# New landing times and biases in a hand-planned instruction order, and gate logits in other buffers, in a gated attention and GEGLU kernel

## Chip, cores and metric

One core of one Trainium2 chip runs the whole program. The metric is the device time of one execution in microseconds (us), lower is better. A profile of one execution gives the "span", from the first to the last instruction on the core; the execution's own time is a little longer than its span. The engines are TensorE (PE; its weight loads are listed as PEld), VectorE (DVE), ScalarE (ACT), GpSimd (POOL) and SyncE (SP). In this program POOL and SP mostly issue DMA transfers; their queues are written POOLq and SPq.

## The reference

The input x is [1, 2048, 1024] in bf16. Two branches read it and a sigmoid gate mixes them row by row:

```
g = sigmoid((x * gate_w).sum(-1))                       # one number for each row
# A: 32 heads of 32; window of 8 keys at distance 2 (s, s-2, ..., s-14)
q, k, v = x @ wqkv                                      # wqkv 1024 x 3072
a = softmax(q . k[window] / sqrt(32)) . v[window] @ wo  # wo 1024 x 1024
# B: GEGLU, 3584 hidden features
b = (gelu(x @ w_gate) * (x @ w_up)) @ w_down
out = g * a + (1 - g) * b
```

## The kernel before

**Tiling.** The 2048 rows are four chunks of 512, handled as two pairs (0, 1) and (2, 3). Each of the three large products (QKV, the FFN's up and gate, and w_down together with wo) is made by one level of a seven-product scheme in the manner of Strassen and Winograd: sums and differences ("forms") of quarters of the operands are made on DVE, and PE makes seven products of them where a plain split needs eight. Partial results pass between the products through PSUM banks: ACT copies a bank to another bank ("seed") or to a float buffer (tags "m5" and "u2", two buffers each), and DVE adds a bank to such a buffer.

**Forms.** T1, T2, T4 are forms of x, made by `x_forms` (T1 on L515, in two halves for the first pair; T2 on L519; the others on L521 and L522). `qkv_forms` (L761) makes the forms of wqkv, once for each pair. `wforms` (L494) makes the forms of w_up and w_gate, which POOL stores to DRAM (L503) for the second pair. `preps` makes the "down sums", forms of w_down and wo: loads by L387 into one of three staging areas in the FFN's hidden buffer hT, four DVE sums to a group (L468 to L473), four stores by POOL (L478). `down_forms` (L1328) makes the forms of the hidden activations.

**PE's stream**, `main`: QKV of the first pair (Q by `first_pair`, matmuls on L595 and L826; K and V by `qkv_pair`, L826); the FFN of chunks 0 and 1 (`ffn`, L1198, 28 blocks of features, f); the down products of chunk 0 (L1367); QKV of the second pair in the order Q, V, K; four blocks of the second FFN; the down products of chunk 1; the rest of that FFN; the down products of chunks 2 and 3. In `qkv_pair` a bank is released to PE by DVE's sums L891 and L901 and by ACT's copies L862, L874, L884 and L912. In `ffn` the sum L1265 (up half) and the sum L1286 (before the second GELU) do so, and L1247 multiplies by the GELU.

**Gate.** `gate(c)` makes the gate's logits by eight small matmuls (L928). For chunk 0 DVE transposes the bank directly (L942); for chunk 1 ACT first copies it (L936) and DVE transposes the copy (L939). The transposed logits `zt` lie in a tile of tag "u2" for chunks 0 and 1, until DVE has picked out the 16 needed columns (`zq`, L946). The second of the first pair's ACT copies into "u2" (L667) needs that tile.

**Attention** runs on DVE, half a chunk (256 rows) at a time, beside PE's products: scores as window products (L999) and additions (L1005); a transposing DMA on SP's queue (L1068); the softmax (L1079 to L1122); ACT spreads the weights (L1128); two transposing DMAs turn them back (L1137); products with v (L1146) and their sums (L1156 to L1164).

**Parking.** The second pair's q, k and v of chunk 3 have no room of their own yet. They are written into the hidden buffer hT, stored to DRAM by POOL (`park`, L781, 1 MB each), and loaded back by SP later (`moves`, L787). The space in hT is overwritten in the meantime by `down_forms` of chunk 1 (L1328) and by the second FFN.

**What sets the order.** Every operation is an `Op` in one of eleven streams (Python generators), and the class `Weave` merges them into one fixed order for each engine by a list scheduler with a cost model: it repeatedly takes the stream whose next operation has the smallest estimated start plus bias. Nothing of that model runs on the chip, except that the instructions of each engine are chained in the order chosen; on the chip each then waits for its semaphores, and whatever stands behind it on its engine waits too. The rule in `run`:

```
b = s[0] if op.due is None or t + self.AHEAD < op.due else 0.0
b = b if op.bias is None else op.bias
if best is None or t + b < best[0]:
    best = (t + b, t, s, op)
```

`s[0]` is the stream's bias and `t` the estimated start; an operation with a due time loses its stream's bias once that time is near. A DMA's estimated landing (`_emit`) is

```
self.pipe = max(self.pipe, t + 1.4) + nbytes / self.RATE
op.end = self.pipe + 1.3 + (op.tail if op.tail > 1.0 else 0.0)
```

so that `tail` is an extra landing time in the model only.

Of the kernel before, what the change touches and what calls it, by code (L numbers as in the profile page):

```python
# [9 lines left out]
ALU = mybir.AluOpType  # L10
# [4 lines left out]
P = 128  # L15
# [4 lines left out]
SC = 512  # L20
# [23 lines left out]
class Weave:  # L44
# [4 lines left out]

    LAT = 0.1  # L50
    RATE = 370e3
    AHEAD = 12.35

    def __init__(self, nc, tc):
        self.nc, self.tc = nc, tc
# [99 lines left out]
def kernel(  # L155
# [65 lines left out]
    QVK = (0, 2, 1)  # L221
    GMAJ = False
    TORD = (0, 1, 4, 5, 2, 3, 6, 7)
    DUE = (80.01, 302.59)
    XR = FT - 12
    ring = persist.tile([P, NG, GR], BF16)
    banks = [psum.tile([P, SC], F32, name=f"ps{i}") for i in range(8)]
# [145 lines left out]
    def load_prep(i0):  # L373
        n = min(2, NPREP - i0)
        kind, src, nr = ("d", B_w_down, FH) if i0 < FH else ("o", A_wo, NTH)
        r0 = i0 if kind == "d" else i0 - FH
        si = i0 // 2 % NSTG

        def fn():
            st = stage(si)  # L380
            for h, r in ((0, r0), (1, nr + r0)):
                if kind == "d":
                    v = src[r * P:(r + n) * P, :].rearrange("(k p) (h n) -> p k h n", p=P, h=2)
                else:
                    v = AP(src.tensor, src.offset + r * D, [[NT * D, P], [D, n], [NW, 2], [1, NW]])
                for k in range(n):
                    nc.sync.dma_start(out=st[:, 2 * h + k], in_=v[:, k])  # L387
        return Op("SP", (4 * n * P * NW * 2, 2.0 * n), fn, [("preps", i0 - 2 * NSTG)] if i0 >= 2 * NSTG else [("qkv", 1, 0, t) for t in range(NT)] if si == 2 else [("pt", KH - 1, 1)] if si == 1 else [("seeded",)],
                  key=("prep", i0))

    def load_block(sup, b, first=()):
        c0, c1 = b * FB * P, (b + 1) * FB * P
# [68 lines left out]
    def preps():  # L461
        for i0 in range(0, NPREP, 2):
            kind, r0, n = ("d", i0, min(2, FH - i0)) if i0 < FH else ("o", i0 - FH, min(2, NPREP - i0))
            st = stage(i0 // 2 % NSTG)
            b11, b12, b21, b22 = st[:, 0:n, 0], st[:, 0:n, 1], st[:, 2:2 + n, 0], st[:, 2:2 + n, 1]
            fo = (b11, b22, b12, b21)
            t = tt(n * NW)
            f0 = dve(t, lambda: V(out=b11, in0=b12, in1=b11, op=ALU.subtract), due=DUE[0] + 2.82 * i0, deps=[("prep", i0), ], lag=1.0)  # L468
            yield f0
            yield dve(t, lambda: V(out=b12, in0=b22, in1=b12, op=ALU.subtract), due=DUE[0] + 2.82 * i0)  # L470
            f1 = dve(t, lambda: V(out=b22, in0=b22, in1=b11, op=ALU.subtract), [f0], due=DUE[0] + 2.82 * i0)
            yield f1
            last = dve(t, lambda: V(out=b21, in0=b21, in1=b22, op=ALU.subtract), [f1], due=DUE[0] + 2.82 * i0)  # L473
            yield last
            dd = (ddram if kind == "d" else odram)[:].rearrange("f p (k n) -> p f k n", n=NW)
            for f in range(4):
                o = Op("POOL", (n * P * NW * 2, 0.8),
                       lambda f=f: nc.gpsimd.dma_start(out=dd[:, f, r0:r0 + n, :], in_=fo[f]), [last],  # L478
                       key=("preps", i0) if f == 3 else None)
                yield o  # L480
            if i0 + 2 == FH:
                w.done[("stored", "d")] = o
            if i0 + 2 == NPREP:
                w.done[("stored", "o")] = o

    def wforms():
        t = tt(GR)
        for b in range(NBLK):
            ops = []
            for f, x_, y_, op in ((0, "U21", "A22", ALU.add), (2, "A11", "U21", ALU.subtract), (1, 0, "A11", ALU.subtract),  # L490
                                  (3, "A12", 1, ALU.subtract)):
                def go(f=f, x_=x_, y_=y_, op=op, b=b):
                    g = ring_take(("w", 0, b, f))
                    nc.vector.tensor_tensor(out=g, in0=ring[:, held[("w", 0, b, x_)], :],  # L494
                                            in1=ring[:, held[("w", 0, b, y_)], :], op=op)
                o = dve(t, go, [("w", 0, b, x_), ("w", 0, b, y_)], key=("w", 0, b, f), lag=0.5, pre=ring_pre,
                        due=DUE[0] + 11.51 * b)
                yield o
                if f == 2:
                    ring_give(("w", 0, b, "U21"), o)  # L500
                if NSUP > 1:
                    yield Op("POOL", (P * GR * 2, 0.6),
                             lambda b=b, f=f: nc.gpsimd.dma_start(out=fdram[b][:, f * GR:(f + 1) * GR],  # L503
                                                                  in_=ring[:, held[("w", 0, b, f)], :]),
                             [("w", 0, b, f)], key=("ws", b, f))

    def x_forms():
        t = tt(KH * SC)
# [221 lines left out]
    def qkv_forms():  # L730
        for sup in range(NSUP):
            c = 2 * sup
            t = tt(D)
            for which in QVK if sup else (0, 1, 2):
# [13 lines left out]
                for f in range(4):  # L748
                    for kt in range(0, KH, 2):
                        def go(f=f, kt=kt, which=which, c=c):  # L750
                            if f != 2:
                                ring_take(("wqf", c, which, f, kt // 2))
                            o, x_, y_, op = ((lambda: form(0, kt), lambda: raw(kt, 1), lambda: raw(kt + KH, 1), ALU.add),
                                             (lambda: form(1, kt), lambda: form(0, kt), lambda: raw(kt, 0), ALU.subtract),
                                             (lambda: raw(kt, 1), lambda: raw(kt, 0), lambda: raw(kt, 1), ALU.subtract),
                                             (lambda: form(3, kt), lambda: raw(kt + KH, 0), lambda: form(1, kt),
                                              ALU.subtract))[f]
                            args = [z() for z in (o, x_, y_)]
                            m = max(len(z) for z in args)
                            for o1, x1, y1 in zip(*[parts(z, m) for z in args]):  # L760
                                V(out=o1, in0=x1, in1=y1, op=op)  # L761
                        dep = raw_keys(c, which, (kt, kt + KH, kt + 1, kt + 1 + KH))
                        if f in (1, 2):
                            dep.append(("wq", c, which, 0, kt))
                        elif f == 3:
                            dep.append(("wq", c, which, 1, kt))
                        if f == 2 and not sup and which == 0:
                            dep.append(("xf", 0, 1))
                        op = dve(t if c < 2 and which != 1 else t + 0.065, go, dep, key=("wq", c, which, f, kt), lag=0.5,
                                 pre=ring_pre if f != 2 else None,  # L770
                                 bias=(0.05, -0.75)[which == 0] if which < 2 and not sup else None,
                                 due=DUE[1] + 13.63 * QVK.index(which) + 2.54 * f if sup else 0.0)
                        yield op
                        w.done["wq", c, which, f, kt + 1] = op

# [3 lines left out]
    def park(which):  # L779
        r = NT * (0, 2, 1)[which]  # L780
        return Op("POOL", (P * NT * SC * 2, 1.0), lambda: nc.gpsimd.dma_start(  # L781
            out=parked[which].rearrange("p (t s) -> p t s", s=SC), in_=hrow[:, r:r + NT, 0:SC]),
            [("tmp", which, t) for t in range(NT)], key=("parked", which))

    def moves(c):
        def back(which, dst, deps):
# [133 lines left out]
    def gate(c):  # L920
# [9 lines left out]
                                     tile_position=(0, 32 * q), skip_group_check=True)  # L930
        o = pe(KT // 4 + 1, go, ([free] if free else []) + dx + [("gcol",)], key=("z", c))
        yield o
        zt = work.tile([P, SC], F32, tag="m5" if c > 1 else "u2", bufs=2, name="zt")
        if c == 1:
            za = work.tile([P, 2 * SC], BF16, tag="gl", bufs=3, name="za")[:].bitcast(F32)
            e = act(0.48, lambda: nc.scalar.copy(out=za, in_=banks[i][:]), [o])  # L936
            yield e
            bank_give(i, e)
            e = dve(0.63, lambda: nc.vector.transpose(out=zt[:], in_=za), [e])  # L939
            yield e  # L940
        else:
            e = dve(0.63, lambda: nc.vector.transpose(out=zt[:], in_=banks[i][:]), [o], bias=-2.0 if c < 2 else None)  # L942
            yield e
            bank_give(i, e)
        zq = small.tile([P, SC // 32], F32, tag="zq", bufs=2, name="zq")
        e = dve(0.1, lambda: nc.vector.tensor_copy(out=zq[:], in_=zt[:].rearrange("p (b j) -> p b j", j=32)[:, :, 0]), [e],  # L946
                key=("zq", c))
        yield e
        zc = small.tile([P, NST], F32, tag="zc", bufs=2, name="zc")
# [528 lines left out]
    def main():  # L1478
# [20 lines left out]
        for part in down(3):  # L1499
            yield from part  # L1500

    w.run([(0.0, main()), (0.0, loads()), (0.0, late_x()), (0.0, moves(3)), (0.6, wforms()), (0.0, down_forms()), (0.02, x_forms()), (1.95, qkv_forms()),
           (1.53, preps()), (0.1, attention()), (0.28, scores())])
    LOG.append(w)


# [28 lines left out]
```

## Time and profile before

| quantity | value |
|---|---|
| three timed runs | 722.01, 721.44, 719.56 us |
| their median | 721.44 us |
| profiled execution, own time | 720.26 us |
| its span on core 0 | 718.5 us |
| granted TensorE clock | 1.00 |
| DMA | 176.84 MB, mean 246 GB/s |

How to read the profile. The page's first part gives the busy time of each engine, its share of the span and its instruction records (a small share of matmul records can be missing). Rows of a timeline read: start in us, busy us, engine, line and operation, output <- inputs by the program's names, shape, number of instructions merged, and in brackets the idle time of the engine before them with what ended it. In a table by stretches each engine has its busy time and records. "DMA share" is the mean busy share of the core's 16 DMA engines. The chain of waits lists, back from the end, what each step waited for. In a DMA's row, "us to landing" counts from its issue. "PE", "DVE" and so on with a line number mean the instruction issued at that line of the kernel; in the changed kernel lines from about L930 on are two further down.

### The profile page before, as it was taken

How to read it: one execution, taken by the hardware profiler on the slowest of the kernel's cores; microseconds unless marked ns; L12 is line 12 of the kernel's file. 1: busy time of each engine (PE TensorE's matmuls, PEld its weight loads, DVE VectorE, ACT ScalarE, POOL GpSimd, SP SyncE). 2: the span in 40 equal slices, each digit the busy share in tenths (PEclk: the TensorE clock that was granted, in tenths of full speed). 3: DMA queues.
4: the chain of work that ended last, by engine and by line, in shares of the span. 5: the costliest groups of instructions: out<-in, count | busy, mean ns of one | idle time of the engine just before them, and what ended most of it. 6: DMA issues, size and time to landing. Idle time of an engine off the chain costs nothing.

```text
span 718.5 us, 9947 instructions
## 1 busy us (share of the span) xinstructions
PE 708.3 (99%) x3305; PEld 345.7 (48%) x3371; DVE 610.9 (85%) x888; ACT 326.9 (45%) x556; POOL 73.9 (10%) x130
## 2 busy tenths in 40 slices
PE   9999999999999999999989999999999999999998
PEld 5566544444444444456654444444444444444444
DVE  4999999999999979899779988899999997839300
ACT  5353675555675522153455323258556655310111
POOL 0030333343211000100000000100000000001000
PEclk9999999999999999999999999999999999999999
DMA  9952989996896799944558899996658756999993
GB/s 271 371 178 74 267 294 306 355 353 203 217 260 213 220 246 345 337 164 146 105 167 272 279 308 358 303 307 186 179 144 190 177 163 159 316 315 354 305 326 111
DMA packets 182835, 176.84 MB, mean 246 GB/s; under 512 B 56320, under 2 KB 138880, under 8 KB 182656
## 3 DMA queue, kind: packets, MB, share of 16 engines
q1 hardware_dynamic: 173168, 145.53, 69.9%
q0 software_dynamic: 9328, 30.42, 11.6%
q8 instruction: 26, 0.43, 0.2%
q10 hardware_dynamic: 288, 0.26, 0.1%
q14 instruction: 25, 0.20, 0.1%
HBM read 132.65 MB, written 31.46 MB: 228 GB/s over the span
## 4 chain that ended last, share of the span: by engine, by line
PE 84%; issue 10%; DVE 3%; DMA 2%; POOL 1%; ACT 0%; DVEq 0%; POOLq 0%; ACTq 0%
PE ps L1198 45%; PE ps L1367 26%; PE ps L826 10%; DMA parked<-hT 1%; PE ps L595 1%; DMA ring<-dforms 1%; DMA ring<-in_B_w_down_dram 1%; PE ps L322 1%; POOL out_dram L1400 0%; PE ps L552 0%; DVE ring L494 0%; DVE u L1286 0%; DVE xbuf L1091 0%; DVE hT L1265 0%; DVE tf L519 0%
## 5 line engine op out<-in xcount | busy, mean ns | idle before, releaser
L1198 PEld LDWEIGHTS <-ring 128*128 128x128 bf16 x1568 | 153.3, 98 | 185.3 <-issue 0.9
L1198 PE MATMUL ps<-lend,ring 128*128 128x512 bf16 x879 | 210.9, 379 | 0.9
L1198 PE MATMUL ps<-tf,ring 128*128 128x512 bf16 x658 | 162.9, 379 | 0.9
L1367 PE MATMUL ps<-ring,hT 128*128 128x512 bf16 (+1 forms) x704 | 159.6, 375 | 0.9
L1367 PEld LDWEIGHTS <-hT 128*128 128x128 bf16 x722 | 70.6, 98 | 82.6 <-DVE xbuf L1005 0.4
L1146 DVE TENSOR_TENSOR xbuf<-xbuf,lend 128x2048 bf16<-128x2048 bf16 x64 | 78.0, 1222 | 15.3 <-DMA xbuf<-xbuf 15.2
L826 PEld LDWEIGHTS <-ring 128*128 128x128 bf16 x512 | 64.7, 127 | 48.5 <-issue 3.1
L999 DVE TENSOR_TENSOR xbuf<-qo,lend 128x2048 bf16<-128x2048 bf16 x64 | 77.0, 1222 | 0.6 <-ACT lend L884 0.6
L1005 DVE TENSOR_TENSOR xbuf<-xbuf 128x2048 bf16<-128x2048 bf16 x56 | 68.4, 1221 | 0.2
L826 PE MATMUL ps<-tf,ring 128*128 128x512 bf16 x250 | 58.1, 379 | 2.5 <-DVE lend L891 1.8
L826 PE MATMUL ps<-lend,ring 128*128 128x512 bf16 x251 | 57.6, 379 | 0.3
L1230 ACT COPY ps<-ps 128x512 f32<-128x512 f32 x56 | 32.0, 572 | 50.9 <-PE ps L1198 50.7
L1274 ACT ACTIVATE gl<-ps 128x512 bf16<-128x512 f32 x56 | 33.6, 600 | 38.3 <-PE ps L1198 37.2
L1408 ACT ACTIVATE ost<-ps,omg 128x512 bf16<-128x512 f32 x15 | 10.3, 688 | 88.4 <-PE ps L1367 88.4
L1367 PE MATMUL ps<-ring,qo 128*128 128x512 bf16 (+1 forms) x193 | 49.1, 375 | 0.2
L1400 POOL DMA_DIRECT2D out_dram<-ost x24 | 13.0, 541 | 338.9 <-ACT ost L1408 249.7
L1247 DVE TENSOR_TENSOR hT<-hT,gl 128x1024 bf16<-128x1024 bf16 x56 | 38.6, 689 | 9.9 <-ACT hT L1240 9.7
L1290 ACT ACTIVATE gl<-u 128x512 bf16<-128x512 f32 x56 | 35.4, 632 | 22.6 <-DVE u L1286 22.0
L503 POOL DMA_DIRECT2D fforms<-ring x56 | 30.7, 549 | 140.8 <-DVE ring L494 134.6
L1286 DVE TENSOR_TENSOR u<-ps,u 128x512 f32<-128x512 f32 x56 | 38.6, 689 | 2.7 <-PE ps L1198 2.5
L1156 DVE TENSOR_TENSOR xbuf<-xbuf 128x2048 bf16<-128x2048 bf16 x32 | 39.1, 1222 | 0.0
L1282 ACT COPY u<-ps 128x512 f32<-128x512 f32 x56 | 32.8, 586 | 13.4 <-PE ps L1198 13.2
(127 smaller groups left out, 681.4 us busy)
## 6 DMA issues: line engine op xcount, KB each, us to landing
ring<-dforms SPq DMA_DIRECT2D x112, 256.0 KB, 4.9
ring<-in_B_w_down_dram SPq DMA_DIRECT2D x84, 256.0 KB, 5.1
ring<-in_B_w_gate_dram SPq DMA_DIRECT2D x56, 256.0 KB, 4.6
fforms<-ring POOLq DMA_DIRECT2D x56, 256.0 KB, 5.6
ring<-fforms SPq DMA_DIRECT2D x56, 256.0 KB, 4.3
ring<-in_B_w_up_dram SPq DMA_DIRECT2D x42, 256.0 KB, 5.2
ring<-in_A_wqkv_dram SPq DMA_DIRECT2D x32, 256.0 KB, 4.0
ring<-oforms SPq DMA_DIRECT2D x32, 256.0 KB, 5.6
```

What stands on the lines that cost most here:

```text
L826: nc.tensor.matmul(banks[bk][:], lhsT=lhsT, rhs=rhs[:, kt, :], start=(start and kt == 0), stop=(kt == KH - 1), skip_group_check=True)
L999: V(out=w3(box[t]), in0=q_b, in1=k_w, op=ALU.mult)
L1005: V(out=w3(box[0]), in0=w3(box[0]), in1=w3(box[t]), op=ALU.add)
L1146: return dve(tt(n), taking(("p", t), lambda: V(out=w3(box["p", t]), in0=w3(box["ab"]), in1=v_w, op=ALU.mult)), [("qkv", c, 2, t), abo] + ( ...
L1156: V(out=p0.rearrange("p (u n) -> p u n", u=2), in0=lo, in1=hi, op=ALU.add)
L1198: nc.tensor.matmul(banks[bk][:], lhsT=wv[:, k, fl * P:(fl + 1) * P], rhs=rhs[:, k, :], start=(start and k == 0), stop=(k == KH - 1), skip_ ...
L1247: yield dve(tt(2 * SC), lambda hv=hv, gv=gv: nc.vector.tensor_tensor(out=hv, in0=hv, in1=gv, op=ALU.mult), [e, ev[f, "g1"], ev[f, "g2"]], ...
L1274: nc.scalar.activation(out=gl[f][:, r1 * SC:(r1 + 1) * SC], in_=banks[A[f]][:], func=ACT.Gelu_apprx_tanh)
L1282: nc.scalar.copy(out=u2[f][:], in_=banks[Bk[f]][:])
L1286: e = dve(tt(SC, True), lambda f=f: nc.vector.tensor_tensor(out=u2[f][:], in0=banks[Dk[f]][:], in1=u2[f][:], op=ALU.add), [o, ev[f, "u2"]])
L1290: ev[f, "g2"] = act(0.54, lambda f=f: nc.scalar.activation(out=gl[f][:, r2 * SC:(r2 + 1) * SC], in_=u2[f][:], func=ACT.Gelu_apprx_tanh), [ ...
L1367: nc.tensor.matmul(banks[bk][:, o0:o0 + cols[1] - cols[0]], lhsT=l, rhs=wv[:, i, cols[0]:cols[1]], start=(start and k == 0), stop=(q == la ...
```

## The change

Numbers of the order model: the look-ahead `AHEAD`, the first due times `DUE`, the slopes of due times, stream biases, and an extra landing time (`tail`) for the loads of the down sums, the stores of FFN weight forms, and the park stores. The operations themselves, their engines and their data stay the same, except that some of L761's forms of 1024 columns are issued as two of 512 where their two operands no longer lie at one distance, and that the buffers and one dependency of the gate are edited: the transposed logits of chunks 0 and 1 go to a tile of tag "gl" (three buffers, otherwise for GELU outputs and results), and chunk 0's transpose waits for the second half of T1, ("xf", 0, 1). The diff, with the first of the four like lines of `preps`:

```diff
-    AHEAD = 12.35
+    AHEAD = 14.59
...
-    DUE = (80.01, 302.59)
+    DUE = (80.05, 297.87)
...
@@ load_prep @@
-                  key=("prep", i0))
+                  key=("prep", i0), tail=3.5)
...
@@ preps @@
-            f0 = dve(t, lambda: V(out=b11, in0=b12, in1=b11, op=ALU.subtract), due=DUE[0] + 2.82 * i0, deps=[("prep", i0), ], lag=1.0)
+            f0 = dve(t, lambda: V(out=b11, in0=b12, in1=b11, op=ALU.subtract), due=DUE[0] + 1.87 * i0, deps=[("prep", i0), ], lag=1.0)
...
@@ wforms @@
-                        due=DUE[0] + 11.51 * b)
+                        due=DUE[0] + 12.15 * b)
...
-                             [("w", 0, b, f)], key=("ws", b, f))
+                             [("w", 0, b, f)], key=("ws", b, f), tail=1.4)
...
@@ qkv_forms @@
-                                 bias=(0.05, -0.75)[which == 0] if which < 2 and not sup else None,
-                                 due=DUE[1] + 13.63 * QVK.index(which) + 2.54 * f if sup else 0.0)
+                                 bias=(0.19, -0.6)[which == 0] if which < 2 and not sup else None,
+                                 due=DUE[1] + 19.19 * QVK.index(which) + 3.94 * f if sup else 0.0)
...
@@ park @@
-            [("tmp", which, t) for t in range(NT)], key=("parked", which))
+            [("tmp", which, t) for t in range(NT)], key=("parked", which), tail=2.6)
...
@@ gate @@
-        zt = work.tile([P, SC], F32, tag="m5" if c > 1 else "u2", bufs=2, name="zt")
+        zt = work.tile([P, SC], F32, tag="m5", bufs=2, name="zt")[:] if c > 1 else \
+            work.tile([P, 2 * SC], BF16, tag="gl", bufs=3, name="ztg")[:].bitcast(F32)
...
-            e = dve(0.63, lambda: nc.vector.transpose(out=zt[:], in_=banks[i][:]), [o], bias=-2.0 if c < 2 else None)
+            e = dve(0.63, lambda: nc.vector.transpose(out=zt, in_=banks[i][:]), [o] + ([("xf", 0, 1)] if c == 0 else []),
+                    bias=-2.0 if c < 2 else None)
...
@@ main @@
-    w.run([(0.0, main()), (0.0, loads()), (0.0, late_x()), (0.0, moves(3)), (0.6, wforms()), (0.0, down_forms()), (0.02, x_forms()), (1.95, qkv_forms()),
-           (1.53, preps()), (0.1, attention()), (0.28, scores())])
+    w.run([(0.0, main()), (0.0, loads()), (0.0, late_x()), (0.0, moves(3)), (0.6, wforms()), (0.0, down_forms()), (0, x_forms()), (1.89, qkv_forms()),
+           (0.12, preps()), (0.03, attention()), (0.23, scores())])
```

More of the change, by code (lines that the diff above doesn't have):

```diff
@@ L467, in preps @@
             t = tt(n * NW)
-            f0 = dve(t, lambda: V(out=b11, in0=b12, in1=b11, op=ALU.subtract), due=DUE[0] + 2.82 * i0, deps=[("prep", i0), ], lag=1.0)
+            f0 = dve(t, lambda: V(out=b11, in0=b12, in1=b11, op=ALU.subtract), due=DUE[0] + 1.87 * i0, deps=[("prep", i0), ], lag=1.0)
             yield f0
-            yield dve(t, lambda: V(out=b12, in0=b22, in1=b12, op=ALU.subtract), due=DUE[0] + 2.82 * i0)
-            f1 = dve(t, lambda: V(out=b22, in0=b22, in1=b11, op=ALU.subtract), [f0], due=DUE[0] + 2.82 * i0)
+            yield dve(t, lambda: V(out=b12, in0=b22, in1=b12, op=ALU.subtract), due=DUE[0] + 1.87 * i0)
+            f1 = dve(t, lambda: V(out=b22, in0=b22, in1=b11, op=ALU.subtract), [f0], due=DUE[0] + 1.87 * i0)
             yield f1
-            last = dve(t, lambda: V(out=b21, in0=b21, in1=b22, op=ALU.subtract), [f1], due=DUE[0] + 2.82 * i0)
+            last = dve(t, lambda: V(out=b21, in0=b21, in1=b22, op=ALU.subtract), [f1], due=DUE[0] + 1.87 * i0)
             yield last
@@ L938, in gate @@
             bank_give(i, e)
-            e = dve(0.63, lambda: nc.vector.transpose(out=zt[:], in_=za), [e])
+            e = dve(0.63, lambda: nc.vector.transpose(out=zt, in_=za), [e])
             yield e
         else:
-            e = dve(0.63, lambda: nc.vector.transpose(out=zt[:], in_=banks[i][:]), [o], bias=-2.0 if c < 2 else None)
+            e = dve(0.63, lambda: nc.vector.transpose(out=zt, in_=banks[i][:]), [o] + ([("xf", 0, 1)] if c == 0 else []),
+                    bias=-2.0 if c < 2 else None)
             yield e
@@ L945, in gate @@
         zq = small.tile([P, SC // 32], F32, tag="zq", bufs=2, name="zq")
-        e = dve(0.1, lambda: nc.vector.tensor_copy(out=zq[:], in_=zt[:].rearrange("p (b j) -> p b j", j=32)[:, :, 0]), [e],
+        e = dve(0.1, lambda: nc.vector.tensor_copy(out=zq[:], in_=zt.rearrange("p (b j) -> p b j", j=32)[:, :, 0]), [e],
                 key=("zq", c))
```

## The prediction

> **What bounds the kernel now.** I read the totals first, then PE's timeline, then for each hole in it the engine named as its releaser. The totals give, for each engine, busy us, share of the span and records:
>
> ```profile
> span 718.5 us, 9947 instructions
> PE 708.3 (99%) x3305; PEld 345.7 (48%) x3371; DVE 610.9 (85%) x888; ACT 326.9 (45%) x556; POOL 73.9 (10%) x130
> ```
>
> PE is the bound, and its clock is 1.00 throughout. The change leaves PE's 3357 matmuls and their order as they are, so time can only come from, or go into, PE's pauses. PE's timeline shows full stretches of 512-column matmuls starting every 0.216 us. A late start is therefore: next start, less last group's start, less issued matmuls times 0.216. (A record in fifty is missing: the "x23" at 361.37 is 24 matmuls by the code.) All pauses that count, in three windows of that timeline (start, us, what, idle before and releaser):
>
> ```profile
> 14.95 1.05 PE L826 MATMUL ps<-tf,ring 128*128 128x512 bf16 x4
> 16.41 1.02 PE L826 MATMUL ps<-tf,ring 128*128 128x512 bf16 x4 [0.41 <-DVE tf L515]
> ...
> 23.12 1.03 PE L826 MATMUL ps<-lend,hT 128*128 128x512 bf16 x4
> 24.47 2.75 PE L826 MATMUL ps<-lend,hT 128*128 128x512 bf16 x12 [0.32 <-ACT u2q L667]
> ```
> ```profile
> 199.25 1.03 PE L1198 MATMUL ps<-tf,ring 128*128 128x512 bf16 x4
> 200.30 1.89 PE L1198 MATMUL ps<-lend,ring 128*128 128x512 bf16 x8
> 202.30 1.89 PE L1198 MATMUL ps<-tf,ring 128*128 128x512 bf16 x7
> ```
> ```profile
> 361.37 5.34 PE L826 MATMUL ps<-lend,ring 128*128 128x512 bf16 x23
> 368.51 1.89 PE L826 MATMUL ps<-tf,ring 128*128 128x512 bf16 x8 [1.79 <-DVE lend L891]
> ```
>
> At 16.41 four matmuls from 14.95 end their turn at 14.95 + 4 x 0.216 = 15.81: 0.60 late. At 24.47: 23.98 was due, 0.49 late. At 200.30: 200.11 was due, 0.19. At 202.30: 202.03 was due, 0.27. At 368.51: 361.37 + 24 x 0.216 = 366.55 was due, 1.96. Together **3.51 us**; the rest of the span offers nothing to gain. Three of the DVE's timelines show the causes:
>
> ```profile
> 15.07 0.72 DVE L942 STREAM_TRANSPOSE zt<-ps 128x512 f32<-128x512 f32 x1 [0.18 <-PE ps L928]
> 15.71 0.65 DVE L515 TENSOR_TENSOR tf<-lend,lend 128x1024 bf16<-128x1024 bf16 x1
> ```
> ```profile
> 121.28 0.69 DVE L468 TENSOR_TENSOR hT<-hT 128x1024 bf16<-128x1024 bf16 x1
> 123.48 0.69 DVE L470 TENSOR_TENSOR hT<-hT 128x1024 bf16<-128x1024 bf16 x1 [1.50 <-DMA hT<-in_B_w_down_dram]
> ...
> 128.95 1.22 DVE L1146 TENSOR_TENSOR xbuf<-xbuf,lend 128x2048 bf16<-128x2048 bf16 x1
> ```
> ```profile
> 365.63 2.22 DVE L1328 TENSOR_TENSOR hT<-hT 128x1792 bf16<-128x1792 bf16 x2 [3.81 <-DMA parked<-hT]
> 367.77 1.28 DVE L891 TENSOR_TENSOR lend<-ps,m5q 128x512 bf16<-128x512 f32 x2
> ```
>
> **The change, part by part.** The new biases and landing times are no instructions; what counts is the order that they give, read from the two built programs.
>
> *Gate logits.* The gate's transpose L942 stood between the two halves of the first form T1; it now waits for the second half. That half follows the first at the DVE's pace of 0.60: 14.20 + 0.60 = 14.80, done near 15.45, before PE's 15.81. So 0.60 goes. Late next could be T2 (L519), moved back by the transpose, not in sum: both still precede it, it ends at about 17.3, and PE reaches its first T2 matmul at about 18.2. The gate's bank comes free at 16.2 instead of 15.8; its next taker is due at 17.3. The second pause: ScalarE's copy L667 stood until 23.83 for the DVE's zq copy L946 at 23.58 (waits: 2.5 us in one), since logits sat in one of the two "u2" buffers which L667 fills. They now sit in "gl", whose three buffers are otherwise used by GELU, first after 66 us. So 0.49 goes. Sum 1.09.
>
> *Cost of split forms.* Seven of L761's 1024-wide sums become pairs of 512-wide ones (888 to 895 DVE records). By their rows (0.689 and 0.422 mean) that is at most 7 x (2 x 0.422 - 0.689) = 1.09 us of DVE, between 24 and 40 us. There the DVE has holes (0.57 at 40.83, two of 0.17 after) and PE none that it causes; I cost it at 0, and at up to 1.09 if a form in that stretch is the one PE is waiting for.
>
> *Down sums (L468 to L473) in FFN 1.* From 66 us the DVE is the crowded engine (columns: PE busy and records, PEld, DVE, ACT, POOL, clock, DMA share, GB/s):
>
> ```profile
> 66.00:86.00 20.00, 19.89 (x93) 11.60 (x94) 19.88 (x28) 9.44 (x18) 3.82 (x7) 1.00 0.65 178
> 86.00:124.00 38.00, 37.84 (x175) 17.22 (x177) 36.19 (x67) 26.64 (x45) 15.31 (x24) 1.00 0.98 308
> 124.00:206.00 82.00, 81.44 (x372) 36.95 (x379) 81.27 (x124) 49.29 (x88) 25.76 (x42) 1.00 0.93 283
> ```
>
> The pauses at 200.30 and 202.30 end an 82 us stretch with 0.73 us of DVE idling: it simply arrives late. Group three, four sums x 0.60 = 2.4 us, moves from 73.9-85.2 to 44-48, where the DVE had two holes of 0.17 and otherwise did products L999 that nobody waits for yet; its operands' last load is issued by 36 and lands within 5.9. Two load waits in L470 (1.9 in all, 1.50 of it shown) also fall away, because group six begins near 126 instead of 121.3 while its loads keep their place. Counting DVE work ahead of the same L1265 in both orders, the new one carries at most 2.0 us more (17th f) and 0.20 to 0.27 at the 19th and at the stage's end. Against it stand the load waits, 1.9, and PE's arrival 1.09 earlier, which the DVE, bound by work and not by PE, does not need to follow in full. 0.46 goes; bounds 0.46 gained to 1.09 lost (all of the early gain eaten because the DVE can't come earlier).
>
> *First attention half, moved earlier.* In before its two turning DMAs L1137 are issued at 105.52 and 114.62, SyncE stands 8.83 us for the first, and the first L1146 runs at 128.95. In after the second turn is issued ahead of a load group and the products L1146 stand right behind the fifth L1265, at about 115.4. Turns go out at about 99.6 and 102.7 (L1128's copies, 104.36 and 107.57 before, come some 6 earlier); even the longest of L1137's landings, 9.2, makes it 111.9. The load group behind, issued from 106.9 before, follows at about 104.2, since SyncE's stand shrinks to some 3 us. Cost 0 with 3.5 us to spare; the price if the cover goes is a rival below.
>
> *Park stage.* The largest pause's cause, in the chain of waits (start, us, what):
>
> ```profile
> 357.27 8.27 DMA parked<-hT
> ```
>
> L1328 overwrites what that store reads, so the DVE stood 3.81 at it, and two ready L891 stood behind. In after both L891 and two L901 precede the first L1328. They run from about 364.2, when PE's sums are there, to 365.6; PE's next group is due at 366.55. So 1.96 goes. Late next: L1328 itself, three of 1.0 us in a row, then the next group's L891 with 0.5 to 1.7 us to spare. A page of the Trainium skill speaks against this part: "SBUF — State Buffer", section "The DMA setup-cost knee (why "@ 1 MiB" ≠ asymptote)", puts a transfer at some 2 us plus bytes over 436 GB/s. By it this 1 MB store would take an estimated 4.4 us and land at 361.7, as the DVE gets to it, the part would be worth nothing and the sum 1.55. The row's 8.27, next to weight loads on the same engines, decides.
>
> *Park loads back (L787) on SyncE's queue.* Three weight loads now pass the first, which stood 389.3 to 392.1; the second, 1 MB, moves ahead of four 256 KB pieces of w_down: 1 MB at 315 GB/s is 3.3 us later for those. They are issued from 397, needed from 416, and land in 5.1: cost 0, up to 3.3 without that cover.
>
> **Sum.** 720.26 (profiled execution; 718.5 span and 1.76 around it) - 0.60 - 0.49 - 0.46 - 1.96 = 716.75. The three timed runs have a median of 721.44; with the profiled execution all four average 720.82, 0.56 above the latter. A median of after should lie 0.56 to 1.18 above its profile: I take 0.65, **717.4 us**, or -0.56%. A measurement of this kernel tells about 0.3%, 2.2 us, from no change: 719.3 to 723.6.
>
> **Rivals.** (1) *FFN 1 eats the early gain.* The DVE is full from 66 to 250 us and can't come earlier; PE's 1.09 is given back at L1265 and 0.46 stays, so only the 1.96 of the park stage remains: 720.26 - 1.96 + 0.65 = 718.95, and 719.5 if half a microsecond of crowding (L1265 of f=17) is added. For: 81.27 of 82. Against: the load waits, and group three's earlier place. (2) *Slower: the turns land late.* At 86 to 124 the DMA engines are 0.98 busy, and w_down loads there take 8.0 (median) against 5 elsewhere. If the second turn lands as late as before, near 123.8, the DVE now stands at L1146 from 115.4 for 8.4 us. The next L1265 then ends at about 128.9 where PE needs it at 123.0: 5.9 us of pause. 720.26 - 3.51 + 5.9 + 0.65 = 723.3, to 724.5 with the early gain eaten too. It decides from a landing after about 117.9, what PE's slack of 2.5 covers. (3) *Nothing real happens*, the model alone changes: 721.4. Against it: DVE order differs at dozens of places.
>
> **Chances.** Forecast and smaller variants under 719.3: 0.60. Rival 1 splits about this bound: 0.20, half each side. Rival 2: 0.17, of which 0.12 is above 723.6. Rival 3: 0.03. Faster 0.70, same 0.18, slower 0.12. The range takes in the forecast, 716.0 (716.75 with the median 0.7 below the profile, as the fastest run of before lies), up to rival 1 and partial losses in the park stage, 720.8.
>
> **What would show it.** Right: PE without holes at 15.8, 23.5-24.4, 199-201 and 362-366; no wait of L1328 for the park store ahead of L891; L470 without load waits. Wrong: the first L1146 with a DMA wait near 115, holes at L1198 released by L1265 between 115 and 206, or L826 after 368 released by L891.

## The result, and the profile after

Over six executions each, the changed kernel has a median of 716.93 us (716.54 to 718.75) and the kernel before 720.82 us (719.56 to 722.01): ratio **0.9952, 95% interval 0.9936 to 0.9968**. Run once more beside other kernels it gave 717.15 us and 0.995 (0.9934 to 0.9966). The profiled execution took 716.74 us, span 715.0: 3.5 us less than before in span. The forecast was 717.4, 716.0 to 720.8.

The totals of the changed kernel, and its chain that ended last by engine:

```profile
span 715.0 us, 10030 instructions
PE 711.0 (99%) x3371; PEld 345.9 (48%) x3371; DVE 611.9 (86%) x895; ACT 328.2 (46%) x556; POOL 73.8 (10%) x130
...
PE 99%; ACT 0%; issue 0%; DVE 0%
```

The chain is nothing but PE now; before it had 84% PE and 16% of issue, DVE, DMA and POOL. (PE's busy time is larger because this trace has all 3371 matmul records, where the one of before has 3305.) The same three windows of PE's timeline:

```profile
14.81 1.90 PE L826 MATMUL ps<-tf,ring 128*128 128x512 bf16 x8
...
22.39 3.62 PE L826 MATMUL ps<-lend,hT 128*128 128x512 bf16 x16
...
198.91 1.89 PE L1200 MATMUL ps<-lend,ring 128*128 128x512 bf16 x8
200.63 1.89 PE L1200 MATMUL ps<-tf,ring 128*128 128x512 bf16 x8
...
359.88 5.34 PE L826 MATMUL ps<-lend,ring 128*128 128x512 bf16 x24
365.06 1.89 PE L826 MATMUL ps<-tf,ring 128*128 128x512 bf16 x8
```

None of the rows has a bracket: eight T1 matmuls run where two groups of four stood 0.60 apart, sixteen where four and twelve stood 0.49 apart. 198.91 + 8 x 0.216 = 200.64, and 359.88 + 24 x 0.216 = 365.06, so those rows follow without a pause. The only new late start of note is 0.18 at 224.98. In DVE's timeline of the park stage the sums now stand ahead of the instruction that waits for the store:

```profile
362.74 0.69 DVE L891 TENSOR_TENSOR lend<-ps,m5q 128x512 bf16<-128x512 f32 x1 [2.35 <-PE ps L826]
363.60 0.69 DVE L891 TENSOR_TENSOR lend<-ps,m5q 128x512 bf16<-128x512 f32 x1 [0.17 <-ACT xbuf L1130]
364.21 1.08 DVE L1330 TENSOR_TENSOR hT<-hT 128x1792 bf16<-128x1792 bf16 x1
```

The DVE idles 2.5 us here instead of 3.8, now for PE instead of for a DMA, and PE is not late. Of the wait of L470 for its loads and of L667 for the gate nothing is left.

### The profile page after: what moved, and what is told of

Read it like the earlier page. It is cut to its first block, busy times and chain, and to the rows that moved or that the text cites. A ratio compares the mean times of both kernels' runs of the same rounds, so it can differ in the third digit from the quotient of the medians.

```text
span 715.0 us, 10030 instructions
## 1 busy us (share of the span) xinstructions
PE 711.0 (99%) x3371; PEld 345.9 (48%) x3371; DVE 611.9 (86%) x895; ACT 328.2 (46%) x556; POOL 73.8 (10%) x130
## 4 chain that ended last, share of the span: by engine, by line
PE 99%; ACT 0%; issue 0%; DVE 0%
PE ps L1200 47%; PE ps L1369 30%; PE ps L826 18%; PE ps L595 2%; PE ps L322 1%; PE ps L552 0%; PE ps L928 0%; PE ps L962 0%; ACT ost L1468 0%; PE ps L557 0%; DVE xbuf L320 0%
## 5 line engine op out<-in xcount | busy, mean ns | idle before, releaser
L1200 PEld LDWEIGHTS <-ring 128*128 128x128 bf16 x1568 | 153.3, 98 | 185.0 <-issue 0.5
L1200 PE MATMUL ps<-lend,ring 128*128 128x512 bf16 x896 | 212.6, 379 | 0.0
L1200 PE MATMUL ps<-tf,ring 128*128 128x512 bf16 x672 | 164.3, 379 | 0.0
L1148 DVE TENSOR_TENSOR xbuf<-xbuf,lend 128x2048 bf16<-128x2048 bf16 x64 | 77.8, 1221 | 15.0 <-DMA xbuf<-xbuf 14.9
L826 PEld LDWEIGHTS <-ring 128*128 128x128 bf16 x512 | 64.9, 127 | 45.8 <-DVE tf L515 0.4
L1007 DVE TENSOR_TENSOR xbuf<-xbuf 128x2048 bf16<-128x2048 bf16 x56 | 68.3, 1220 | 0.3
L826 PE MATMUL ps<-tf,ring 128*128 128x512 bf16 x256 | 58.2, 379 | 0.0
L826 PE MATMUL ps<-lend,ring 128*128 128x512 bf16 x256 | 57.9, 379 | 0.0
L1288 DVE TENSOR_TENSOR u<-ps,u 128x512 f32<-128x512 f32 x56 | 38.5, 688 | 3.9 <-PE ps L1200 3.5
L494 DVE TENSOR_TENSOR ring<-ring 128x1024 bf16<-128x1024 bf16 x56 | 38.4, 685 | 1.9 <-DMA ring<-in_B_w_up_dram 1.9
```

What stands on the lines that cost most here:

```text
L826: nc.tensor.matmul(banks[bk][:], lhsT=lhsT, rhs=rhs[:, kt, :], start=(start and kt == 0), stop=(kt == KH - 1), skip_group_check=True)
L1007: V(out=w3(box[0]), in0=w3(box[0]), in1=w3(box[t]), op=ALU.add)
L1148: return dve(tt(n), taking(("p", t), lambda: V(out=w3(box["p", t]), in0=w3(box["ab"]), in1=v_w, op=ALU.mult)), [("qkv", c, 2, t), abo] + ( ...
L1200: nc.tensor.matmul(banks[bk][:], lhsT=wv[:, k, fl * P:(fl + 1) * P], rhs=rhs[:, k, :], start=(start and k == 0), stop=(k == KH - 1), skip_ ...
L1288: e = dve(tt(SC, True), lambda f=f: nc.vector.tensor_tensor(out=u2[f][:], in0=banks[Dk[f]][:], in1=u2[f][:], op=ALU.add), [o, ev[f, "u2"]])
```

## The experiments

A changed number of the planner can move instructions everywhere. So in every kernel below (but the repeat of the changed one) the planner's choices were written down and replayed, and single entries of that list were moved; all other instructions keep their place on their engine:

```diff
-        while live:
-            best = None
...
+        for z in ORDER:
+            s = next(y for y in live if y[3] == int(z, 16))
+            op = s[2] if isinstance(s[2], Op) else s[2]()
+            t = None if op is None else self._start(op)
```

The list in front moves the line numbers by 22 to 26 (L848 is L826, L492 is L470, L1222 is L1198 or L1200). "Hole" is PE's lateness, as in the prediction: time between two starts less 0.216. "Order of" says whose order was frozen. Each ratio is to the kernel before, from several executions; spans and holes are of one profiled execution each.

| run | order of | span | ratio (95%) | holes after 18 us, of 0.15 or more |
|---|---|---|---|---|
| early_alone | before | 717.9 | 0.9984 (0.9975-0.9993) | 0.25, 0.30, 0.19 (129-166), 0.18, 0.29 (200, 202), 1.35 (368) |
| three_moves | before | 717.4 | 0.9970 (0.9960-0.9981) | 0.63, 0.19 (140, 166), 0.18, 0.29, 0.86 (380) |
| three_moves_g3 | before | 717.6 | 0.9965 (0.9952-0.9978) | 1.27, 0.19 (140, 166), 0.18, 0.29, 0.86 |
| three_moves_load | before | 717.5 | 0.9968 (0.9956-0.9980) | 0.18, 0.44, 0.32 (123-130), 0.18, 0.18, 0.86 |
| five_moves | before | 716.8 | 0.9977 (0.9967-0.9987) | 0.22, 0.32 (127-129), 0.18, 0.18, 0.83 (390) |
| six_moves | before | 717.1 | 0.9974 (0.9965-0.9984) | 0.36, 0.32 (127-129), 0.18, 0.83 (390) |
| changed_again | changed | 715.1 | 0.9950 (0.9934-0.9966) | 0.19 (225) |
| no_gate_part | changed | 715.6 | 0.9968 (0.9956-0.9981) | 0.17 (24) |
| park_undone | changed | 716.9 | 0.9978 (0.9968-0.9987) | 1.35 (367) |
| g3_late | changed | 717.0 | 0.9970 (0.9960-0.9981) | 0.47, 0.97 (91-95), 0.24, 0.25 (225-227) |
| late_turn | changed | 721.2 | 1.0047 (1.0034-1.0060) | 4.49 (125) |
| late_products | changed | 720.1 | 0.9992 (0.9981-1.0002) | 2.66 (136), 0.19, 0.25 (228-230) |

The five runs from three_moves to six_moves can't be told apart by their ratios (0.9965 to 0.9977, each known to about 0.001), and the intervals of no_gate_part and g3_late overlap that of changed_again. What is said of single moves below therefore rests on one profiled execution each.

### Parts of the change, put into the order of before

**The gate part alone (early_alone)**

```diff
 DVE
   L515 first half of T1
-  L942 transpose of the gate's bank
   L515 second half of T1
+  L942 transpose of the gate's bank
```

(and the "gl" tiles of the change's diff).

> The kernel before with its order frozen, and only the gate part of the change: the transposed logits in "gl" tiles, and the transpose L942 behind the second half of T1. Nothing else moves on any engine. Theory (each pause is worth its own lateness): PE's holes at 16.4 (0.60) and 24.5 (0.49) are gone, the rest arrives 1.09 earlier and the holes near 199 and 201 (0.46) and 367 (1.96) stay as they are: span 718.5 - 1.1 = 717.4, ratio to before 0.9985. Rival (FFN 1 is bound by the DVE's work and eats the early gain): the first two holes are gone but those near 199 to 201 grow from 0.46 to about 1.5, span 718.5, ratio 1.000.

The holes at 16.4 and 24.5 are gone, and PE reaches the first pair's FFN ("FFN 1") 0.76 earlier (the gate's sums, small matmuls just ahead of it, start at 57.47 instead of 58.23). But PE's timeline at the end of the first FFN's crowded stretch reads:

```profile
200.30 1.89 PE L1222 MATMUL ps<-lend,ring 128*128 128x512 bf16 x8
202.31 1.89 PE L1222 MATMUL ps<-tf,ring 128*128 128x512 bf16 x8
```

Before had 200.30 and 202.30: **all of it was given back** in new holes at 129, 139 and 166. In the profile the rival is right for this order. (The 0.6 by which the span is shorter comes at 368, where the park store happened to land 0.6 sooner.) The times speak for the theory: its 0.9985 lies inside the interval of 0.9975 to 0.9993, the rival's 1.000 outside. What the executions without a profile gained, and where, isn't shown; a faster park store in them would do it as well.

**The park stage with it (three_moves)**

```diff
 DVE
-  L1328, L1328, L891, L891, L901, L1328, L901
+  L891, L891, L1328, L901, L901, L1328, L1328
```

> The kernel before with its order frozen, the gate part, and one more swap: two L891 and two L901 ahead of the L1328 that waits for the park store. Theory: 0.60 + 0.49 + 1.96 = 3.05 gone, holes near 199 to 201 stay at 0.46; span 715.4, ratio 0.9958. Rival (FFN 1 eats the early gain): 1.96 gone, span 716.5, ratio 0.9973. A second rival for the park stage (the next thing is late instead: L1328, or the L891 after it): a new hole in L826 or L1198 after 367, and less than 1.0 of the 1.96 gained.

Up to 291 us nothing is gained here either (the gate matmuls of the second pair, the first work behind FFN 1 and the down products of chunk 0, start at 291.38; before 291.31). Then 1.96 goes at 368 and 0.86 comes back at 380, by PE's timeline and DVE's ahead of it:

```profile
379.56 1.89 PE L848 MATMUL ps<-tf,ring 128*128 128x512 bf16 x8 [0.70 <-DVE lend L913]
```
```profile
371.88 3.49 DVE L1023 TENSOR_TENSOR xbuf<-qo,lend 128x2048 bf16<-128x2048 bf16 x3
...
378.82 1.28 DVE L913 TENSOR_TENSOR lend<-ps,m5q 128x512 bf16<-128x512 f32 x2
```

Six instructions, three of them score products (L1023, 3.4 us), stand ahead of the next L913 here; in the changed order four do, one of them a score product. So both rivals hold: 1.96 - 0.86 = 1.1, which is the whole difference of the spans, 718.5 - 717.4.

**The third group of down sums, earlier (three_moves_g3)**

```diff
 DVE, POOL
-  group 3: L468, L470, L471, L473 and four stores L478 at 73 to 95 us
+  the same at 43 to 52 us
```

> As the run with three moves, and the third group of down sums (four DVE sums and their four stores) moved from 73 to 85 us to where the changed kernel has it, 43 to 48 us; everything else in the order of before. Theory A (the holes near 199 to 201 come from 2.4 us of DVE work too many after 66 us): they go, span 714.9 to 715.0, the changed kernel's own. Theory B (they come from the two load waits of L470, which stay here): they stay at 0.46, span 715.4, and the DVE idles longer at L470 near 121, by about the 2.4 us that it is ahead.

The DVE's 2.4 us are spent earlier, and lost again two steps on. DVE's timeline, waits for loads in L492 (before: 1.50 and 0.35):

```profile
122.11 0.69 DVE L492 TENSOR_TENSOR hT<-hT 128x1024 bf16<-128x1024 bf16 x1 [1.41 <-DMA hT<-in_B_w_down_dram]
...
136.12 0.69 DVE L492 TENSOR_TENSOR hT<-hT 128x1024 bf16<-128x1024 bf16 x1 [1.97 <-DMA hT<-in_B_w_down_dram]
```

Theory A falls: the holes near 200 are unchanged, and the one at 140 is twice as large. By this trace the stage is held in this order by what the DVE waits for.

**The loads of groups six and seven, earlier (three_moves_load)**

```diff
 SP
-  turn L1137, weights of block 4, down loads of group 6, turn L1137, weights of block 5, down loads of group 7
+  down loads of group 6, turn L1137, weights of block 4, down loads of group 7, turn L1137, weights of block 5
```

> The run with three moves, and on SyncE's queue the loads of the sixth and the seventh group of down sums put ahead of the weight loads of their block and of the turn that stood before them; DVE's order is untouched. Theory B (FFN 1 ends where the load waits of L470 put it, so PE's early gain of 1.09 and the holes near 139, 200 and 202 all hang on them): no wait of that line above 0.3, those holes gone, the stage's end 1.0 to 1.5 earlier, the hole near 379 (0.86) stays; span 715.9 to 716.4, ratio 0.9965. Rival C (the DVE's work, not the loads, binds): the waits go but a DVE-late hole takes their place by 202; span 717.4, ratio 0.998 to before as the run with three moves.

L492 no longer waits, but L518 (the weight forms, L494) does:

```profile
115.22 0.69 DVE L518 TENSOR_TENSOR ring<-ring 128x1024 bf16<-128x1024 bf16 x1 [0.39 <-DMA ring<-in_B_w_up_dram]
119.70 0.69 DVE L518 TENSOR_TENSOR ring<-ring 128x1024 bf16<-128x1024 bf16 x1 [2.06 <-DMA ring<-in_B_w_gate_dram]
```

Together 2.45, where three_moves had 2.75 in L492. The wait changed its line, not its size; theory B falls in this form, as C does.

**Two sums more (five_moves), and the third group too (six_moves)**

```diff
 DVE
-  L1005, L1146, L891, L891
+  L891, L891, L1005, L1146
```

> As the run with three moves and the loads, and the next two L891 after the park stage ahead of one score addition and one score product. Theory (the pauses and the two things behind them are all that the new order is worth): the hole near 379 goes as well, span 715.0 to 715.5, ratio 0.995, as the changed kernel with its 351 moved DVE instructions. Rival (other moves of the new order matter too): holes remain in FFN 1 or after 367, span above 716.

> As the run with five moves, and the third group of down sums with its stores early, at 43 to 48 us. Theory D (the waits between 115 and 136 come from transfers: the DMA engines are full from 96 on, and both moves are needed, the stores out of 86 to 96 and the loads of the sixth and seventh group ahead of the turn that holds SyncE's queue): the DVE's waits for loads between 110 and 140 fall from 1.8 to 3.4 us to below 0.7, no holes in FFN 1, span 715.0 to 715.6. Rival E (the weight loads behind the turn stay where they are, and with them the end of the stage): waits of 1.5 us or more for block weights or for down loads remain and the holes near 200 and 202 too, span 716.5 to 717.

The hole at 380 goes, and one of 0.83 at 390 comes. At the hole of 0.32 at 129, what PE's own row names in both runs is a load of the gate weights (0.15 and 0.16). In FFN 1 the DVE still waits 2.05 and 2.19 us for loads, and the next gate matmuls start 0.5 and 0.2 us earlier than in before (290.82 and 291.12; 291.31). So rival E holds in the main: the old order stays 1.8 us of span behind the new one with five moves, and 2.1 with all six.

### The changed order, with one thing undone

**The gate part (no_gate_part)**

```diff
 DVE
   L515 first half of T1
+  L942 transpose of the gate's bank
   L515 second half of T1
-  L943 transpose of the gate's bank
```

(and "u2" tiles again).

> The changed kernel with its order frozen and only the gate part undone: logits in "u2", the transpose L942 between the halves of T1. Nothing else differs. Theory (in the new order FFN 1 doesn't bind, so what PE loses at the start it keeps): holes of 0.6 near 15.8 and 0.5 near 24 come back, none is given back in FFN 1, span 716.0 to 716.2. Rival (FFN 1 binds here too, the gate part is worth nothing by the end): span 715.0 to 715.3.

The gate sums start at 57.81 instead of 57.02, 0.79 late, and the next gate matmuls at 290.44 instead of 289.82: 0.62 of the loss is still there behind FFN 1, and the span is 0.6 longer. So in this order, other than in the old one, most of what is lost at the start reaches the end (park_undone, below, loses 0.58 up to 57 us for no reason in its edit, and 0.61 is there at 290). The gate part's own share is smaller than expected: 0.34 at 16.3 and 0.17 at 24.0. A third hole, 0.48 at 15.1, belongs to a wait that the gate part has no hand in, and is part of the 0.6:

```profile
15.10 1.02 PE L848 MATMUL ps<-tf,ring 128*128 128x512 bf16 x4 [0.31 <-DVE tf L537]
16.30 1.02 PE L848 MATMUL ps<-tf,ring 128*128 128x512 bf16 x4 [0.18 <-DVE tf L537]
```

**The park stage (park_undone)**

```diff
 DVE
-  L891, L891, L1330, L901, L901, L1330
+  L1330, L1330, L891, L891, L901, L901
```

> The changed kernel with its order frozen, and only two L1330 put back ahead of the two L891, where they wait for the park store. Theory: the DVE stands 3 to 5 us at L1330 from about 361 and the hole of 1.96 comes back in L826 near 367, by as much as the store lands after 363 (8.3 us after its issue near 355.5 would be 363.8: a hole of 1 to 2); span 716 to 717. Rival (the page's estimate, a store of 1 MB in 4.4 us): it lands near 360, no hole, span 715.0.

DVE's and PE's timelines:

```profile
364.15 2.22 DVE L1352 TENSOR_TENSOR hT<-hT 128x1792 bf16<-128x1792 bf16 x2 [3.14 <-ACT xbuf L1152]
```
```profile
367.02 1.89 PE L848 MATMUL ps<-tf,ring 128*128 128x512 bf16 x8 [1.19 <-DVE lend L913]
```

The row names ACT, but the park store was issued at 356.4 and took 7.7 us: it landed at 364.1, where L1352 starts. The hole is 1.35. (The other 0.6 of the span is there before 57 us already: 0.58.)

**The third group of down sums (g3_late)**

```diff
 DVE, POOL
-  group 3 with its stores at 43 to 52 us
+  group 3 with its stores at 73 to 95 us
```

> The changed kernel with its order frozen, and only the third group of down sums put back to where it ran before, 73 to 85 us, with its stores. Theory (2.4 us of DVE work put into a stretch in which the DVE had some 1.2 us of idling left up to 124): the DVE runs 1 to 2 us later at 124 and later; the holes near 199 to 201 come back with 0.3 to 1.0, span 715.4 to 716. Rival (the third group's place is worth nothing, as it was in the order of before): span 715.0 to 715.2, the DVE's idle time between 66 and 206 merely shrinks.

There are 1.44 us of holes at 91 and 95, where PE waits for the DVE, and 0.3 more near 225 than in the changed kernel. From the gate sums to the next gate matmuls PE takes 234.65 us (57.23 to 291.88) instead of 232.80 (57.02 to 289.82): the group's place is worth **1.85**. The DVE is late, as expected, by somewhat more and not at 200.

**The second turn (late_turn)**

```diff
 SP
-  turn, turn, weights of block 4, down loads
+  turn, weights of block 4, down loads, turn
```

> The changed kernel with its order frozen, and only the second turn L1139 of the first attention half put back behind the five loads that it was moved past. Rival 2 of the prediction, its price measured: the turn is issued some 4 to 8 us later and lands between 114 and 120; the DVE stands at the first L1148 (114.4) until then. If it lands before about 117.9 PE loses nothing; beyond that, each us of it is a us of PE pause at L1200 released by L1267, up to 2. A cost above 3 us would mean that the slack of 2.5 was overrated.

DVE's and PE's timelines:

```profile
121.59 1.23 DVE L1170 TENSOR_TENSOR xbuf<-xbuf,lend 128x2048 bf16<-128x2048 bf16 x1 [6.83 <-DMA xbuf<-xbuf]
```
```profile
125.09 3.19 PE L1222 MATMUL ps<-lend,ring 128*128 128x512 bf16 x8 [4.32 <-ACT m L1280]
```

This is rival 2. The DVE starts L1148 at 121.59 instead of 114.42, 7.17 later; PE, which arrives 0.26 later than in the changed kernel, loses 4.49: its cover is 2.4 (2.5 by the prediction). The turn landed later, at 121.5, and cost more than this run's expectation had (by 120, up to 2). PE loses 1.7 more behind the hole, since the granted clock is 0.58 in the next 3 us: 16 matmuls take 5.14 instead of 3.46. The three executions without a profile were slower still (724.4 to 724.8, this one 723.0).

**Three attention instructions (late_products)**

```diff
 DVE
-  L1148 at 114.4, L1148 at 120.3, L1158 at 122.1
+  all three behind 126 (they ran at 128.4 to 132.0), ahead of the third L1148
```

> The changed kernel with its order frozen, and only three DVE instructions, the first two products L1148 of the first attention half and their sum L1158 (3.4 us together), moved from 114 to 123 us to one place behind 126. Loads, turns and all else as they are. Theory F (the earlier turn is worth something because it gives the DVE other work while the loads for L494 and L470 are still on their way, in a stretch with full DMA engines): the DVE now stands for loads, 1.5 us or more between 114 and 127, and these 3.4 us come on top later: a hole of 0.5 to 2 us in FFN 1, span 715.5 to 717. Rival G (loads are in time by themselves in the new order, the work's place is free): waits below 0.5, no hole above 0.3, span 715.0 to 715.3.

The DVE idles for 4.0 us between 115 and 127 and has the same 3.4 us to do later:

```profile
115.89 0.69 DVE L1310 TENSOR_TENSOR u<-ps,u 128x512 f32<-128x512 f32 x1 [0.93 <-PE ps L1222]
...
121.93 0.69 DVE L1310 TENSOR_TENSOR u<-ps,u 128x512 f32<-128x512 f32 x1 [1.21 <-PE ps L1222]
...
127.19 0.69 DVE L516 TENSOR_TENSOR ring<-ring 128x1024 bf16<-128x1024 bf16 x1 [1.18 <-DMA ring<-in_B_w_up_dram]
```
```profile
135.54 3.16 PE L1222 MATMUL ps<-lend,ring 128*128 128x512 bf16 x8 [2.50 <-ACT m L1280]
```

A hole of 2.66, 1.7 of slow clock behind it (16 matmuls from 135.54 to 140.68), and 5.1 us of span in this execution, of which 0.46 is there before 57; by the times hardly anything is left of the change's gain (0.9992). Theory F is right in its direction; the loss is larger than it had, and its mechanism isn't shown: only 1.18 of the 4.0 are a wait for loads, the rest are waits for PE's own sums and once for ACT (0.46). And the edit does two things. It takes ready work away between 114 and 123, and it puts 3.4 us in one piece ahead of the sum L1310 (L1288). ACT waits for that sum, and its copy L1280, which PE waits for, stands behind:

```profile
128.40 2.35 DVE L1170 TENSOR_TENSOR xbuf<-xbuf,lend 128x2048 bf16<-128x2048 bf16 x2
130.79 1.23 DVE L1180 TENSOR_TENSOR xbuf<-xbuf 128x2048 bf16<-128x2048 bf16 x1
132.05 1.22 DVE L1170 TENSOR_TENSOR xbuf<-xbuf,lend 128x2048 bf16<-128x2048 bf16 x1
133.19 0.68 DVE L1310 TENSOR_TENSOR u<-ps,u 128x512 f32<-128x512 f32 x1
```

In the changed kernel that sum starts at 128.09. A run with the three instructions spread out behind it was not made.

### The changed kernel again

> The changed kernel once more, beside the others on the same chip. Span 715.0, time 716.5 to 717.1 for most executions; two of its first six lay at 718.5 and 718.8, and if such an execution is profiled, one hole of about 1.8 us should be seen that the first profile hasn't got.

The profiled execution lies at 716.92 and has no large hole, so what the executions near 718.5 (and one of 719.55 here) lose isn't shown.

## Why the prediction was right, and where it was not

**The sum was right**: the five holes went, 3.51 us of them, and the span fell by 3.5. That it fits to 0.1 us is in part luck, since the parts differ by more: PE reaches the gate sums 1.21 earlier (1.09 in the sum) and gains 0.28 from there to 290 (0.46). The median lies 0.2 above the profiled execution, not the 0.65 that were added: that is the 0.5 between 717.4 and 716.93. (The matmuls number 3371, not 3357; nothing in the sum hangs on it.)

**Gate logits, 1.09: right in the trace, mis-sized as a part.** Undone by itself in the new order it brings back 0.51 of holes. The step that failed is the 0.60 for the transpose between the halves, worked out as if only the second half could be late. In ten of the twelve runs PE stands 0.3 to 0.7 for the first half already, at 15, and in nine of these L515 itself waits 0.2 to 0.4 for the load of x. Neither trace shown at first (before and changed) has that hole: there the load of x landed at 14.17 and 13.89, in the ten runs at 14.0 to 14.6. Why it lands differently no run settles.

**FFN 1, 0.46 gained and 1.09 not eaten: right for the changed kernel, and the reasons given were not enough.** Rival 1 is what happens in the old order: early_alone ends the stage at 202.31 as before does. The third group alone (three_moves_g3) only lengthens the load waits, and loads alone (three_moves_load) only move them. In the new order the third group's place is worth 1.85 (g3_late). The prediction had the waits of L470 go because group six would begin near 126 while its loads keep their place. That step failed, though the waits went: the group begins at 123.21, and its loads land earlier, the last at 121.6 instead of 123.4. For group seven it is 130.1 instead of 135.7.

**The first attention half, "cost 0": looked at only as a risk, and its worth stays open.** Its turns are issued at 99.7 and 101.4, and were at 105.5 and 114.6, where the second stood in SyncE's queue ahead of weight loads and of group seven's. So the move can help in two ways: loads behind the turns land earlier, and the DVE has products ready at 114, where in the old order these come from 129 on, with 1.9 to 3.4 us of DVE waits between 115 and 136 and a DVE that is full from there to 250. By late_products 3.4 us of that work, put late in one piece, cost nearly the whole gain; how much of it is the piece's place, that run can't tell. No kernel here made this move alone in the old order; that one of the two, or both, is what the six moves lack is argued from the two orders, not shown.

**Rival 2**: place and cover (2.4 against 2.5) were right. The price was low: by its rule, a microsecond for each after 117.9, a landing at 121.5 costs 3.6, and 4.49 was measured, as the DVE comes to the products at 114.4 and not at 115.4; the clock's 1.7 was missed. That it didn't come was due to the order on SP's queue, where the two turns stand together: put one back, and 0.5% gained is 0.5% lost.

**Park stage, 1.96: right for this profile.** Two L891 but no L901 precede the first L1328 in the changed order, other than the prediction read; it did no harm, as the store had landed at 363.4. With the old order of this stage 1.35 was measured twice (early_alone, park_undone), where the store took 7.7 us. The 8.27 of the kernel before is the longest of the fourteen profiles, whose median is 7.7, so 1.96 is more than the part is usually worth. The named next thing, "the next group's L891 with 0.5 to 1.7 us to spare", is what three_moves ran into with 0.86 in the old order; the changed order has fewer products there. The Trainium skill's 2 us plus bytes over 436 GB/s ("SBUF — State Buffer", section "The DMA setup-cost knee (why "@ 1 MiB" ≠ asymptote)"), an estimated 4.4 us for this store, would have made the part worth nothing. This store landed after 7.5 to 8.3 in all profiles, beside weight loads on the same engines.

**Split forms and the loads back, 0 each: right**: no hole between 24 and 57, none between 379 and 551 of more than 0.1 in the changed kernel.

## What to carry to other kernels

List the late starts of the bounding engine, not its waits or its busy share: here five numbers gave the new span to 0.1 us. Then undo each part by itself, since parts can be off in both directions while the sum fits. What one repair is worth depends on the stages behind it: by the traces, 0.76 gained at the start was given back in one order, and 0.62 of 0.79 lost there reached the end of FFN 1 in the other. When work on a full engine moves earlier, price the transfer that it hangs on for coming late.

## What the runs showed of the hardware that was not expected

PE's granted clock fell after pauses that are not long. In late_products the pause was 2.50 us; the table by stretches behind it (columns as in the prediction's table) reads:

```profile
133.00:135.50 2.50, 0.05 (x1) 0.00 (x0) 2.50 (x5) 1.60 (x4) 0.73 (x2) 1.00 0.07 21
135.50:138.70 3.20, 3.15 (x9) 1.19 (x9) 3.17 (x6) 0.97 (x2) 3.20 (x5) 0.58 0.98 284
138.70:141.00 2.30, 2.30 (x11) 0.96 (x9) 2.30 (x4) 1.06 (x2) 0.05 (x1) 0.85 1.02 365
```

After 1.79 us (before, at 368.5) the clock stayed at 1.00. So here the pauses of 2.50 us and of 4.32 (late_turn) cost 1.7 us more than themselves, and one of 1.79 did not; where between them this begins, and whether the length alone decides, isn't shown. Nine of the eleven executions of late_products have a mean granted clock of 1.00 and the profiled one 0.997, so most of them seem to have been spared. "TensorE: Matmul & The Clock Gate", section "What's actually happening", of the Trainium skill has the clock halved after an idle window of about 3.4 us; here 2.5 was enough.
